# RWKV-7 state update without zero products, and MoE tail products in 64x64 tiles behind one step of the recurrence

## The chip, the cores and the metric

The kernel runs on one core of a Trainium2 chip. The metric is the device time of one execution in microseconds. An engine of the core runs its own list of instructions in order and waits for the others at semaphores: TensorE (PE; its weight loads are listed apart, as PEld), VectorE (DVE), ScalarE (ACT), GpSimd (POOL) and SyncE (SP), which issues nearly all the DMAs. PE multiplies a stationary operand, loaded by one instruction, with a moving one, streamed through by the next. A product that needs fewer than 128 rows or columns of the array can be put in a smaller tile (64x64, 32x64, ...), and products in different tiles run side by side. An fp32 product appears in the trace as two rows, each with its own weight load.

## The reference

Two blocks follow each other. The first is a recurrence over 768 steps, for 4 batches and 8 heads with a 40x40 state each:

```python
for t in range(S):
    y[:, :, t] = einsum('bhd,bhde->bhe', rt, state)
    Sa = einsum('bhde,bhe->bhd', state, at)
    state = state * wt - einsum('bhd,bhe->bhde', Sa, bt)
    state = state + einsum('bhd,bhe->bhde', vt, kt)
```

Its output, turned to 3072 tokens of 320 numbers, goes through the second block (the MoE): `h = x @ w_in` (320 to 2048), `g = h * cos(h)`, `g @ w_out` (2048 to 320). The second block's weights are float64 in memory; the kernel rounds them on the chip.

## The kernel before

The recurrence is cut into 24 chunks of 32 steps. With 4 batches this fills the 128 partitions: a block of 32 partitions for each batch (`blk`), or two halves of 64 partitions for the two heads of a pair (`half` takes the 40 used rows of each, `full` all 64). Within a chunk the recurrence is matrix algebra, and the chunk's main steps, in order, are t (transposes of the state, tile `sT`), q (the old state times r, tile `qps`), x (tile `x0ps`), s (tile `sps`) and z (the state update, tile `dps`, function `ch_z`). Steps v, k and g (tiles `vT`, `kT`, `gram`) prepare the next chunk from r, k and v; the p1 steps (`wT`, `aps`, `bT`, `nps`) and a triangular inverse on DVE prepare further ahead.

In z the result of one chunk is summed in four PSUM banks, one for each batch: products with kn (k divided by the decay), products with bn, and, ahead of both, eight products of a tile of bf16 zeros (`idle`), 64 wide and 288 columns long. They open the sum for all 64 partitions of each half: kn and bn products write 40 of the 64, and DVE (lines 736 and 743) reads all 128 partitions. Both kn and bn buffers are 64 columns wide with zeros in columns 40 to 63 (`kept("kn", ...)` fills the padding once).

The second block's work is cut into pieces: for each of 12 groups of 256 tokens and each of 4 slices of 512 hidden columns, a first half in two pieces, `first_a` and `first_b` (products in tile `ph`), then the cosine on ACT and DVE (lines 810 to 820), then the second half in two pieces (`second`, tile `po`). The 320 inputs are two full blocks of 128 rows and a tail of 64 rows. The tail's products (`tails`, with `w_in_tail`) use 64 rows and 128 columns of the array, for e = 0 and 1 in the upper and lower half of the rows, and write two PSUM banks.

The order is written out by hand: a list `segs` for each chunk names the steps, and a mark M stands where a piece of the MoE goes. `step` runs one step, notes in `G["small"]` whether it was one of the steps with small tiles (q, x, g, s, z and a few others), and issues what was put off (`later`), which holds the DMAs. `first_b` looks at that note: if the step just before it was small, the tail's products come first and the full ones after them; else the other way round. All PE products go through the helper `mm` at line 101, so groups are told apart by their tiles. Some products of zeros stand elsewhere only to keep PE going (`busy`, `spare`, FILL), and at chunk 19 there are 75 products of one column (`pad`).

Three waits hang on the places in question: ACT line 810 reads `ph` when a piece's first half is done; ACT line 654 copies q's result into `qz`, which x reads; DVE lines 736 and 743 read `dps` after z, POOL scales the state, and the next t reads it.

## Time and profile before

| what | value |
|---|---|
| time, median of 3 runs | 814.49 us (811.71 to 815.90) |
| the profiled execution's own time | 814.53 us |
| its span, first to last instruction | 812.8 us |
| mean granted TensorE clock | 0.975 |
| PE busy | 758.7 us (93%), 17,859 products |
| DVE / ACT / POOL busy | 485.8 / 387.1 / 199.4 us |
| products of zeros in z (`dps<-idle`) | 192 rows, 8.3 us busy |
| tail products (`ph<-xT,w_in_tail`) | 384 rows, 54.7 us busy |
| kn products (`dps<-vvm,kn`) | 1,536 rows, 21.6 us busy |
| reads of instructions (queue q8) | 140 packets of 16 KB |

A row of the list of groups gives line, engine, operation, output<-input, the shape, the count, the busy time in us and the mean of one in ns. A row of the timeline gives start and length in us of instructions of one kind merged together; since products side by side overlap, the time that a group takes is read from its start to the next group's start. "[0.45 <-issue]" behind a row says that the engine stood idle 0.45 us before it while it waited for nothing that the profile shows. The view of busy time by stretches gives for each engine its busy time in that stretch.

### The profile page before, as it was taken

Reading aid. Unit: us, or ns where it says so; the run is one execution under the profiler, and the core shown is the slowest. Engines: PE = TensorE matmul, PEld = TensorE weight load, DVE = VectorE, ACT = ScalarE, POOL = GpSimd, SP = SyncE. Lnnn points to the kernel's source line nnn. Section 1 sums busy time; section 2 is a strip of 40 time slices with the busy share of each in tenths; the row PEclk is TensorE's granted clock in tenths of the full one; section 3 lists DMA queues with packets and bytes.
Section 4 is the critical chain, followed back from the end, with each engine's and each line's share of the span. In section 5 each row is a group of like instructions: output and inputs, shape, how many; then the busy total and the mean of one; then the engine's idle time right before and its main releaser. Section 6 shows DMA issues by size and latency. Waiting matters only on the chain.

```text
span 812.8 us, 39682 instructions
## 1 busy us (share of the span) xinstructions
PE 758.7 (93%) x17859; PEld 582.0 (72%) x17859; DVE 485.8 (60%) x1025; ACT 387.1 (48%) x723; POOL 199.4 (25%) x354
## 2 busy tenths in 40 slices
PE   3678799799999999999999999999999999999997
PEld 2545477677777777777777777777777777777775
DVE  6948858855743797553895554994346873332231
ACT  1326577454454346446436535534635445363352
POOL 5215634330404230230330330331130222201000
PEclk9878699999999999999999999999999999999999
DMA  8656553344244324324214314223220212101000
GB/s 123 120 142 170 158 141 99 54 114 67 51 94 92 67 42 72 69 89 70 59 36 74 78 47 71 55 45 68 45 45 21 45 37 57 23 14 36 19 17 16
DMA packets 183304, 55.79 MB, mean 69 GB/s; under 512 B 157152, under 2 KB 178656, under 8 KB 183136
## 3 DMA queue, kind: packets, MB, share of 16 engines
q1 hardware_dynamic: 180560, 51.95, 29.5%
q8 instruction: 140, 2.29, 1.2%
q10 hardware_dynamic: 2320, 0.98, 0.6%
q0 software_dynamic: 256, 0.33, 0.2%
q14 instruction: 28, 0.23, 0.1%
HBM read 42.07 MB, written 11.14 MB: 65 GB/s over the span
## 4 chain that ended last, share of the span: by engine, by line
PE 68%; DVE 15%; DMA 4%; issue 4%; ACT 4%; SPq 3%; POOL 1%; DVEq 0%; ACTq 0%; POOLq 0%
PE ph L101 23%; PE po L101 19%; PE x0ps L101 4%; PE dps L101 3%; DVE inv_tmp L478 3%; SPq L152 3%; PE gram L101 3%; DVE inv L482 3%; PE vT L328 2%; DVE rw L393 2%; PE sps L101 2%; PE busy L101 2%; PE nps L101 2%; PE qps L101 2%; PE sT L638 1%
## 5 line engine op out<-in xcount | busy, mean ns | idle before, releaser
L101 PE MATMUL po<-w_out_sb,gT 128*128 128x320 f32 x768 | 223.3, 439 | 0.0
L101 PE MATMUL ph<-xT,w_in_sb 128*128 128x256 f32 x768 | 186.7, 388 | 1.5 <-DMA xT<-xd 1.5
L101 PEld LDWEIGHTS po<-w_out_sb,gT 128*128 128x128 f32 x768 | 140.2, 190 | 54.2 <-issue 1.7
L101 PEld LDWEIGHTS ph<-xT,w_in_sb 128*128 128x128 f32 x768 | 140.5, 191 | 30.0 <-issue 10.6
L810 ACT ACTIVATE turns<-ph,rnd 128x512 f32<-128x512 f32 x96 | 64.1, 686 | 151.7 <-PE ph L101 151.3
L812 DVE SCALAR_TENSOR_TENSOR turns<-turns,ph 128x512 f32<-128x512 f32 x96 | 64.0, 684 | 116.0 <-ACT turns L810 115.8
L820 DVE TENSOR_TENSOR gT<-ph,turns 128x512 f32<-128x512 f32 x96 | 65.8, 686 | 37.8 <-ACT turns L817 37.8
L737 POOL TENSOR_TENSOR qz<-qz,wc 128x160 f32<-128x160 f32 x92 | 42.0, 475 | 158.5 <-DVE qz L736 157.9
L817 ACT ACTIVATE turns<-turns,half_pi 128x512 f32<-128x512 f32 x96 | 69.3, 722 | 3.1
L816 ACT ACTIVATE turns<-turns 128x512 f32<-128x512 f32 x96 | 60.1, 627 | 19.1 <-DVE turns L812 19.1
L101 PE MATMUL ph<-xT,w_in_tail 64*128 64x256 f32 x384 | 54.7, 402 | 0.0
L482 DVE TENSOR_TENSOR inv<-inv,inv_tmp 128x31 f32<-128x31 f32 (+15 forms) x124 | 51.2, 413 | 4.3
L570 POOL COPY vp<-nat_v 128x320 f32<-128x320 f32 x24 | 11.7, 489 | 164.4 <-DMA nat_v<-in_v_dram 121.1
L478 DVE TENSOR_TENSOR inv_tmp<-u,inv 128x31 f32<-128x31 f32 (+15 forms) x124 | 48.5, 391 | 2.3
L736 DVE TENSOR_TENSOR qz<-dps,qz 128x160 f32<-128x160 f32 x92 | 29.1, 316 | 33.3 <-PE dps L101 33.2
L393 DVE RECIPROCAL rw<-nat_w 128x320 f32<-128x320 f32 x20 | 42.8, 2142 | 0.0
L642 ACT COPY s<-sT 128x512 f32<-128x512 f32 x46 | 24.5, 585 | 37.8 <-PE sT L638 37.8
L101 PEld LDWEIGHTS ph<-xT,w_in_tail 64*128 64x128 f32 x384 | 33.3, 186 | 9.3 <-issue 5.6
L101 PEld LDWEIGHTS <-idle 32*64 32x64 bf16 (+2 forms) x443 | 21.5, 101 | 24.3 <-issue 19.7
L748 POOL TENSOR_TENSOR yt<-yt,wb 128x512 f32<-128x512 f32 x24 | 31.6, 1316 | 22.4 <-DVE yt L743 22.4
L702 DVE TENSOR_TENSOR sm<-sps,su 128x128 f32<-128x128 f32 x48 | 11.7, 285 | 34.1 <-ACT sm L697 31.3
L394 POOL TENSOR_TENSOR bn<-nat_b,rw 128x320 f32<-128x320 f32 x22 | 19.8, 900 | 48.5 <-DVE rw L393 38.5
(136 smaller groups left out, 1126.7 us busy)
## 6 DMA issues: line engine op xcount, KB each, us to landing
words<-in_moe_w_in_dram SPq DMA_DIRECT2D x8, 512.0 KB
nat_k<-in_k_dram SPq DMA_DIRECT2D x96, 40.0 KB
nat_v<-in_v_dram SPq DMA_DIRECT2D x96, 40.0 KB
nat_r<-in_r_dram SPq DMA_DIRECT2D x96, 40.0 KB
xd<-yt SPq DMA_DIRECT2D x48, 80.0 KB
out_dram<-ot SPq DMA_DIRECT2D x24, 160.0 KB
nat_b<-in_b_dram SPq DMA_DIRECT2D x88, 40.0 KB
nat_a<-in_a_dram SPq DMA_DIRECT2D x80, 40.0 KB
```

Source lines behind the costliest of these rows:

```text
L101: nc.tensor.matmul(o, lhsT=lhsT, rhs=rhs, start=start, stop=stop, skip_group_check=True)
L393: nc.vector.reciprocal(rw, wn)
L478: nc.vector.tensor_tensor(tmp, u[:, j : j + 1, :j].to_broadcast([P, C - j, j]), x[:, j:, j : j + 1].to_broadcast([P, C - j, j]), ALU.mult,)
L482: nc.vector.tensor_tensor(x[:, j:, :j], x[:, j:, :j], tmp, ALU.subtract)
L736: nc.vector.tensor_tensor(z, pick(dp, 0, (2 * N72 + C, 2), (N72, 2), (1, D)), z, ALU.add)
L737: nc.gpsimd.tensor_tensor(z, z, wc.rearrange("p (f m b) -> p f m b", f=2, m=2)[:, :, :, bb] .unsqueeze(3).to_broadcast([P, 2, 2, D]), ALU. ...
L748: nc.gpsimd.tensor_tensor(yt.rearrange("p j b t -> p (j b) t"), yt.rearrange("p j b t -> p (j b) t"), wx, ALU.mult)
L810: nc.scalar.activation(n, u, ACTF.Identity, bias=rnd, scale=1.0)
L812: nc.vector.scalar_tensor_tensor(n, n, -ROUND, u, ALU.add, ALU.subtract)
L816: nc.scalar.activation(n, n, ACTF.Abs)
L817: nc.scalar.activation(n, n, ACTF.Sin, bias=half_pi, scale=-2.0 * math.pi)
L820: nc.vector.tensor_tensor(gT[:, 2 * e : 2 * e + 2].rearrange("p f t -> p (f t)"), us[e], ns[e], ALU.mult)
```

## The change

In `ch_z` the eight products of zeros go. The kn products take all 64 columns of kn (`DP` in place of `D`) and write all 64 partitions of a half, and those of j = 0 open the sum. The bn products stay 40 wide.

In `first_b`, where the step just before was q, each tail product 128 columns wide becomes two of 64 columns, in 64x64 tiles. `G["small"]` holds the kind of the step for that; after other small steps the tail's products stay as they were. In the instruction order of the changed program this is so in 16 places, and each has 8 products in place of 4.

The program's PE list goes from 36,027 instructions to 35,922: 384 fewer for the zeros, 256 more for the tails, 23 more waits. The order of everything else, on every engine and in the DMA queues, is the same. Constants (FILL, the 75 `pad` products) are not changed.

```diff
-        G["small"] = small
+        G["small"] = small and G["kind"]
...
-        for bb in range(B):
-            for e in range(2):
-                mm(
-                    ps[bb // 2][full[e], bb % 2, : 4 * N72], idle[blk[bb], :DP],
-                    pick(idle[blk[bb]], 0, (0, 4), (1, N72)), True,
-                )
         for s, n in ((0, kn_b[c % 2]), (1, bn_b[c % 7])):
             for j in range(4):
                 o = C - C * (j // 2)
                 for bb in range(B):
                     for e in range(2):
                         mm(
-                            ps[bb // 2][half[e], bb % 2, j * N72 : (j + 1) * N72],
-                            n[blk[bb], 2 * j + e, :D],
+                            ps[bb // 2][(half if s else full)[e], bb % 2, j * N72 : (j + 1) * N72],
+                            n[blk[bb], 2 * j + e, : D if s else DP],
                             sm[e][blk[bb], j, :] if s else vvm[c % 2][blk[bb], 2 * j + e, o : o + N72],
-                            False,
+                            not s and j == 0,
                         )
...
         def tails(fresh):
             for f in range(2):
                 for e in range(2):
-                    mm(
-                        phs[e][:, f, :], w_in_tail[full[e], j, f, :], xT[full[e], 2, :],
-                        fresh and e == 1 and f == 0, False,
-                    )
+                    for to in (full if G["small"] == "q" else [every]):
+                        mm(
+                            phs[e][to, f, :], w_in_tail[full[e], j, f, to], xT[full[e], 2, :],
+                            fresh and e == 1 and f == 0, False,
+                        )
...
+                    G["kind"] = "q" if seg is q else "other"
```

## The prediction

> **What bounds the kernel now.** I read the page's head first, then the chain that ended last, then busy time by stretches, and then the timeline around one q and one z.

> ```profile
> span 812.8 us, 39682 instructions
> PE 758.7 (93%) x17859; PEld 582.0 (72%) x17859; DVE 485.8 (60%) x1025; ACT 387.1 (48%) x723; POOL 199.4 (25%) x354
> PEclk9878699999999999999999999999999999999999
> ...
> PE 68%; DVE 15%; DMA 4%; issue 4%; ACT 4%; SPq 3%; POOL 1%; DVEq 0%; ACTq 0%; POOLq 0%
> ```

> ```profile
> 62.00:115.00 53.00, 44.51 (x1251) 30.12 (x1251) 41.23 (x74) 33.36 (x59) 29.03 (x29) 0.81 0.59 155
> 115.00:174.00 59.00, 53.09 (x1218) 42.30 (x1217) 44.86 (x82) 35.89 (x65) 22.59 (x35) 0.97 0.40 102
> 174.00:300.00 126.00, 119.77 (x3415) 94.05 (x3414) 78.79 (x176) 59.90 (x117) 27.72 (x55) 1.00 0.35 70
> 300.00:450.00 150.00, 148.00 (x3560) 115.60 (x3559) 97.67 (x212) 72.39 (x136) 34.84 (x63) 1.00 0.33 66
> 450.00:600.00 150.00, 148.99 (x3562) 116.74 (x3561) 92.12 (x196) 73.70 (x138) 38.25 (x71) 1.00 0.27 56
> ```

> In the stretches the first figure after the length is PE's busy time. Up to 174 us PE waits for loads, DVE and others, and the clock is not full; from 300 us it stands still for about 1% of the time, at full clock. A microsecond of PE saved after 174 us is a microsecond of the kernel, nearly; one saved before is perhaps none. Both edits touch PE alone. PE's busy share does not say what a group takes; that is read from start to start:

> ```profile
> 431.38 0.81 PE L101 MATMUL qps<-rT,s 40*40 40x32 f32 x64
> 432.13 1.14 PE L101 MATMUL ph<-xT,w_in_tail 64*128 64x256 f32 x8
> 433.19 1.99 PE L101 MATMUL ph<-xT,w_in_sb 128*128 128x256 f32 x8
> 435.02 0.60 PE L328 MATMUL kT<-ident,kn 128*128 128x128 f32 x4
> 435.55 0.88 PE L101 MATMUL x0ps<-vvm,ag 32*32 32x72 f32 x64
> 436.37 0.89 PE L101 MATMUL x0ps<-qz,aT 40*32 40x72 f32 x64
> 437.18 2.42 PE L101 MATMUL po<-w_out_sb,gT 128*128 128x320 f32 x8
> ...
> 447.36 0.33 PE L101 MATMUL dps<-idle 32*64 32x288 bf16 x8
> 447.51 0.86 PE L101 MATMUL dps<-vvm,kn 32*40 32x72 f32 x62
> ...
> 448.99 1.13 PE L101 MATMUL ph<-xT,w_in_tail 64*128 64x256 f32 x8
> 450.06 1.99 PE L101 MATMUL ph<-xT,w_in_sb 128*128 128x256 f32 x8
> 451.98 1.29 PE L101 MATMUL nps<-aT,bT 40*32 40x32 f32 x128
> ```

> **Term 1, the tails behind q (16 places).** Eight full products take 1.83 us when whole-array products follow (433.19 to 435.02), and 1.92 when small tiles follow (450.06 to 451.98). So a change of tile shape costs 0.09 us at the end of a group: the array drains. It costs again at the start, where the first weight load has no product to hide under:

> ```profile
> L101 PE MATMUL ph<-xT,w_in_tail x384: 375/376/481, 113.3 to 798.1; 64*128 64x256 f32 x192
> ```

> The slowest row is 481 ns against 376, 0.105 us more, and in the records of single instructions those are the first ones of a group. A tail group is then four steps of 0.216 us (the distance of full products' starts), two rows abreast, plus 0.10 at the start and 0.09 at the end: 1.06, as 432.13 to 433.19 shows. Behind q, whose tiles are 64x64, 64x64 tails change no shape: the drain behind q goes (0.09) and the load slides under q's last products (0.10). The four steps stay, now with four rows abreast; q's own rows run four abreast. Gain 0.19 us in each place, 3.0 in all. All 16 lie between 184 and 638 us. What was waiting gets its data earlier (ACT line 810); x reads q's copies 2.9 us after the last of them ends (432.26 plus 1.17 against 436.37), so 0.2 less slack there costs nothing. Bounds: nothing gained would be 0. If the eight extra rows queued one behind the other, each would cost what a row of the 75 `pad` products costs (632.40 to 634.35, 26 ns): 0.2 a place, 3.3 lost. Rows in different tiles of one step start 7 ns apart in the records, so I stay with 3.0 gained.

> **Term 2, the zeros in z (24 places).** They take 447.36 to 447.51, 0.15 us, and z as a whole 1.63. Against a gain of 0.15 speaks x: 128 rows of the same length, no zeros, also 1.63 (435.55 to 437.18), although with one change of tile shape inside. The single starts say why z may not shrink by the whole: its first 32 rows or so run at the array's pace (8 rows each 62 ns), then the queue of issued instructions is empty and the other 104 take 1.14 us, 11 ns each, as issue delivers them. Eight rows fewer are then 8 x 11 = 0.09 us. I take 0.09, between 0 and 0.15, as nearest to how the rows behind the zeros run. Four of the 24 places lie before 174 us; behind two more (207.5 and 239.8 us) PE waits in the same group for ACT (0.36 us) or just after it for DVE (1.4), and stands there longer instead. Left are 18 x 0.09 = 1.6 us; bounds 0 and 24 x 0.15 = 3.5.

> The kn products get wider. Output columns cost no streaming time; the weight load grows. Rows of loads:

> ```profile
> L101 PEld LDWEIGHTS ph<-xT,w_in_sb 128*128 128x128 f32 x768 | 140.5, 191 | 30.0 <-issue 10.6
> L101 PEld LDWEIGHTS dps<-vvm,kn 32*40 32x40 f32 x1536 | 20.2, 112 | 0.0
> ```

> Between 112 ns (40 columns) and 191 (128) lie about 133 for 64: 21 ns more. A tile gets one load each 62 ns, while the product before it streams; hidden, it costs nothing, and I take that. If it showed in each of the 8 rounds of a z, 0.17 us, 18 x 0.17 = 3.0 lost. [...]

> The first kn product now carries the waits that the first zero product carried (for the readers of the PSUM banks on ACT and DVE); 23 of them become instructions of their own. Behind them queues all of PE, but they ended at the same places before, so I count nothing.

> **Term 3, reads of instructions.** PE's program is read in 140 blocks of 16 KB, 256 instructions each:

> ```profile
> q8 instruction: 140, 2.29, 1.2%
> ...
> 443.99 0.69 PE L101 MATMUL sps<-x,rt 32*32 32x72 f32 x42 [0.45 <-issue]
> ```

> Such stops without a releaser (also 1.08 us before 129.90, 0.45 before 169.67, 0.47 before 200.18, and smaller ones, 3.9 us lost in all after 115 us) come in the records at PE's instruction numbers that are 194 above a multiple of 256, 1.3 to 1.5 us after a block has landed. A read starts some 1.0 to 1.3 us after the block before was entered and takes 0.9 to 1.6: where 256 instructions pass in under about 3.7 us, PE stops. The change moves the borders of all later blocks against the work, by up to 105 instructions. Laying the new order's borders over the old times gives a similar set of stops with one more near 205 us. I take 0.8 us lost; bounds 3.9 gained (none left) and 5 lost.

> **Sum.** 3.0 + 1.6 - 0.8 = 3.8 us gained. The profiled execution took 814.53 us, at the median of 814.49; 814.5 - 3.8 = 810.7.

> **Rivals.**
> - *Only the tails count.* z is paced by issue to its end, as x's equal 1.63 suggests, and the zeros were free: 3.0 - 0.8, time 812.3. Against it: fewer instructions have to be issued, too.
> - *Everything comes through.* 0.15 in 18 places, 3.0 for the tails, no new stops: 814.5 - 5.7 = 808.8; with the four early places and some stops gone, 807.
> - *Slower: the instruction blocks.* Each stop shown costs 0.45 to 1.08 us. If the borders fall before the dense stretches (g, x, s with 256 instructions in 1.2 to 1.6 us), about one in 20 of the 110 blocks after 174 us stopping for 1 us more would eat the 4.6 gained; at 9 new stops of 1 us the time is 819. It decides from 5 new ones on. For it: every border behind the first z moves. Against it: most blocks take 5 us or more to pass.
> - *The change does not do what it says*, if the four 64x64 rows of a step do not run abreast: with 0.2 lost in each place, 814.5 + 3.3 - 1.6 + 0.8 = 817.

> **How the numbers follow.** Half a per cent, 4.1 us, is about what a measurement of this kernel tells from no change: its three runs alone span 811.7 to 815.9. The forecast's own range, with terms 2 and 3 varied, is 808.5 to 812.5, chance 0.48, and its middle lies just inside half a per cent, so I split it 0.23 faster, 0.25 same. Only the tails: 0.22, same. Everything: 0.18, faster. Blocks: 0.08, rows not abreast: 0.04, of which 0.02 together still fall within half a per cent. Faster 0.41, same 0.49, slower 0.10. The range takes in all but the ends of these: 806.5 to 815.8. A stretch of half clock more or less before 174 us (one is 3.4 us long) would move the time by up to 1.7 us, and lies in it.

> **What would show it.** Right: tails behind q start about 0.1 us sooner behind q's last row, in eights of four, and the group takes about 0.95 us; no row of 481 ns left among them; z from first kn row to the next group 1.54 in place of 1.63; stops without releaser 4 to 5 us in all. Wrong: tails behind q at 1.06 or more; kn's rows more than 62 ns a round; z at 1.63 or at 1.48; new stops of a microsecond where g or x begins.

## The result, and the profile after

| | before | after |
|---|---|---|
| time, median of 6 runs | 813.91 us (811.71 to 815.90) | 825.28 us (819.46 to 830.80) |
| ratio | | 1.0137, 95% interval 1.0108 to 1.0167 |
| the profiled execution's own time | 814.53 us | 822.18 us |

The change makes the kernel 1.4% slower. The page's head, and the shares of the chain that ended last, for the kernel after:

```profile
span 820.5 us, 39577 instructions
...
PE 757.4 (92%) x17795; PEld 577.4 (70%) x17795; DVE 486.1 (59%) x1025; ACT 386.9 (47%) x723; POOL 199.3 (24%) x354
...
PEclk9968799999899999999999999999999999999999
...
PE 68%; DVE 15%; issue 5%; DMA 5%; ACT 5%; POOL 1%; SPq 1%; DVEq 0%; ACTq 0%; POOLq 0%
```

Sixty-four products fewer, PE busy 1.3 us less, and the span 7.7 us longer: PE does not work longer, it stands longer. Busy time by stretches says where:

```profile
115.00:174.00 59.00, 50.66 (x1162) 39.90 (x1149) 44.27 (x82) 35.81 (x65) 24.40 (x37) 1.00 0.43 112
174.00:300.00 126.00, 115.77 (x3126) 89.85 (x3125) 71.23 (x156) 55.06 (x108) 25.53 (x51) 0.96 0.35 68
300.00:450.00 150.00, 147.28 (x3593) 114.78 (x3594) 103.44 (x225) 73.85 (x139) 33.57 (x60) 1.00 0.32 63
450.00:600.00 150.00, 146.67 (x3598) 114.28 (x3583) 87.20 (x190) 73.53 (x139) 33.93 (x65) 1.00 0.29 58
```

Between 174 and 300 us PE was busy 119.8 us before and is busy 115.8 now, and the clock, 1.00 before, is 0.96. The edits' own places look as they should. PE's timeline around one q and one z of after:

```profile
438.01 0.81 PE L101 MATMUL qps<-rT,s 40*40 40x32 f32 x64
438.65 1.14 PE L101 MATMUL ph<-xT,w_in_tail 64*64 64x256 f32 x16
439.72 1.99 PE L101 MATMUL ph<-xT,w_in_sb 128*128 128x256 f32 x8
...
453.46 0.95 PE L101 MATMUL dps<-vvm,kn 32*64 32x72 f32 x62
...
455.92 0.70 PE L101 MATMUL dps<-sm,bn 32*40 32x72 f32 x41 [1.27 <-issue]
456.55 1.14 PE L101 MATMUL ph<-xT,w_in_tail 64*128 64x256 f32 x8
```

q and its tails take 1.71 us where they took 1.81; this z, alone, is stopped for 1.27 us in its middle by nothing that the profile shows. Such stops fill PE's list of waits after 174 us (who waited, for what, us in total, times, longest):

```profile
PE gram L101 <- issue: 3.0, 2, 2.1
...
PE dps L101 <- issue: 2.0, 2, 1.3
PE nps L101 <- issue: 1.8, 1, 1.8
PE below L101 <- issue: 1.6, 1, 1.6
...
PE sps L101 <- issue: 0.4, 1, 0.4
```

The same list for the kernel before:

```profile
PE below L101 <- issue: 0.5, 1, 0.5
PE sps L101 <- issue: 0.4, 1, 0.4
```

8.8 us against 0.9. All seven stand at PE's instruction numbers 194 above a multiple of 256, or one beside it, 1.2 to 1.6 us after a read of a 16 KB instruction block has landed. Such a place, where PE goes from one block of 256 instructions to the next, is called a border below. Two of them are followed by something dearer. PE's timeline of after:

```profile
198.34 0.31 PE L101 MATMUL below<-rn,noff 32*32 32x16 f32 x14 [1.57 <-issue]
198.58 3.51 PE L101 MATMUL ph<-xT,w_in_sb 128*128 128x256 f32 x8
...
218.27 0.19 PE L101 MATMUL gram<-rT,vT 40*32 40x32 f32 x1 [2.14 <-issue]
```

The eight `ph` products take 3.51 us where before they take 2.00 (196.76): the clock has halved. Busy time in windows of 3.41 us (the last three figures are the clock, the DMA share and GB/s):

```profile
171.57:174.98 3.41, 2.10 (x82) 1.74 (x81) 0.24 (x1) 2.05 (x4) 3.35 (x7) 1.00 0.60 211
174.98:178.39 3.41, 2.63 (x68) 2.19 (x68) 0.81 (x1) 1.89 (x5) 0.35 (x1) 1.00 0.29 74
195.46:198.87 3.41, 1.83 (x130) 1.57 (x130) 0.29 (x1) 0.59 (x2) 0.00 (x0) 1.00 0.42 69
198.87:202.28 3.41, 3.41 (x27) 2.29 (x33) 0.00 (x0) 0.10 (x1) 0.00 (x0) 0.50 0.39 73
215.94:219.35 3.41, 1.11 (x31) 0.86 (x18) 0.42 (x1) 0.37 (x1) 2.73 (x4) 1.00 0.18 53
219.35:222.76 3.41, 2.92 (x75) 2.48 (x73) 3.22 (x4) 0.00 (x0) 0.00 (x0) 0.50 0.23 61
222.76:226.17 3.41, 3.41 (x11) 2.78 (x10) 3.27 (x6) 1.07 (x2) 2.66 (x3) 0.50 0.51 79
```

The two stops that fall into one window (1.83 us busy, 1.11) are followed by half clock. The stop of 1.81 us ahead of 175.76 us, cut in two by an edge (2.10 and 2.63 busy), is not; PE's timeline has it as:

```profile
175.76 0.69 PE L101 MATMUL nps<-aT,bT 40*32 40x32 f32 x58 [1.81 <-issue]
```

**Where the time went.** Laid group by group on the kernel before, from 170 us on, after loses 9.4 us: gained about 3.5 at z and behind q, lost 3.9 in the three half-clock windows (`ph` at 198.6 us 1.52, `sT` and `ph` at 221 and 223 us 0.83 and 1.52), and the rest, some 9 by subtraction, most of it in the stops listed. Up to 170 us it is 1.8 us ahead. That figure varies: e2, e6 and e7 below, whose program up to 165 us is that of before, are 2.4 to 6.6 us ahead of the same profile there. 9.4 - 1.8 = 7.6 is the difference of the two profiled times.

### The profile page after: what moved, and what is told of

Read it like the earlier page. It is cut to its first block, busy times and chain, and to the rows that moved or that the text cites. A ratio compares the mean times of both kernels' runs of the same rounds, so it can differ in the third digit from the quotient of the medians.

```text
span 820.5 us, 39577 instructions
## 1 busy us (share of the span) xinstructions
PE 757.4 (92%) x17795; PEld 577.4 (70%) x17795; DVE 486.1 (59%) x1025; ACT 386.9 (47%) x723; POOL 199.3 (24%) x354
## 3 DMA queue, kind: packets, MB, share of 16 engines
q8 instruction: 140, 2.29, 1.2%
## 4 chain that ended last, share of the span: by engine, by line
PE 68%; DVE 15%; issue 5%; DMA 5%; ACT 5%; POOL 1%; SPq 1%; DVEq 0%; ACTq 0%; POOLq 0%
PE ph L101 22%; PE po L101 20%; PE x0ps L101 4%; PE dps L101 3%; PE gram L101 3%; PE vT L328 2%; DVE rw L393 2%; PE sps L101 2%; DVE inv_tmp L478 2%; DVE inv L482 2%; PE qps L101 2%; PE nps L101 2%; PE busy L101 1%; PE sT L638 1%; DVE turns L807 1%
## 5 line engine op out<-in xcount | busy, mean ns | idle before, releaser
L101 PE MATMUL po<-w_out_sb,gT 128*128 128x320 f32 x768 | 223.3, 439 | 0.0
L101 PE MATMUL ph<-xT,w_in_sb 128*128 128x256 f32 x768 | 188.0, 390 | 1.2 <-DVE gT L815 1.2
L101 PEld LDWEIGHTS po<-w_out_sb,gT 128*128 128x128 f32 x768 | 140.2, 190 | 54.3 <-issue 1.7
L101 PEld LDWEIGHTS ph<-xT,w_in_sb 128*128 128x128 f32 x768 | 141.3, 192 | 31.0 <-issue 12.9
L101 PE MATMUL ph<-xT,w_in_tail 64*128 64x256 f32 (+1 forms) x512 | 54.0, 393 | 0.0
L101 PEld LDWEIGHTS ph<-xT,w_in_tail 64*128 64x128 f32 (+1 forms) x512 | 31.7, 160 | 9.2 <-issue 5.6
L626 ACT COPY vvm<-gram 128x256 f32<-128x256 f32 x24 | 8.8, 368 | 46.8 <-DVE ag L621 46.4
```

Of the source, the lines that this page charges most:

```text
L101: nc.tensor.matmul(o, lhsT=lhsT, rhs=rhs, start=start, stop=stop, skip_group_check=True)
```

## The experiments

Theory: the edits gain what was predicted; the moved borders of PE's 256-instruction blocks cost more than that. Rivals: the new rows themselves are dear; the start-up is upset. "Numbers" are places in PE's list of instructions; a one-column product is two of them.

### e1 and e2: each edit alone

e1 has the change in `ch_z` only, e2 the change in `tails` only.

e1 against before:

```diff
-        for bb in range(B):
-            for e in range(2):
-                mm(
-                    ps[bb // 2][full[e], bb % 2, : 4 * N72], idle[blk[bb], :DP],
...
-                            n[blk[bb], 2 * j + e, :D],
+                            n[blk[bb], 2 * j + e, : D if s else DP],
...
-                            False,
+                            not s and j == 0,
```

e2 against before:

```diff
-        G["small"] = small
+        G["small"] = small and G["kind"]
...
+                    for to in (full if G["small"] == "q" else [every]):
+                        mm(
+                            phs[e][to, f, :], w_in_tail[full[e], j, f, to], xT[full[e], 2, :],
...
+                    G["kind"] = "q" if seg is q else "other"
```

> Only the first edit: the products of zeros are gone, kn's products are 64 columns wide, the tails are as before. Theory (block borders): PE gains 0.08 us in each z, about 1.5 in all, but PE's instruction numbers run 62 to 76 behind those of before between 174 and 240 us, nearly as in the changed kernel (60 to 45 behind), so that stops of 1.5 us and more come there too and are paid a second time by a stretch of half clock: 816 to 823 us. Rival 1 (the rows themselves: wider kn products are dear in a way that the groups' start-to-start times do not show): also slower, 820 to 825. Rival 2 (only the start-up, before 115 us, moved): 812 to 815. The trace tells the first two apart: stops without a releaser and half clock between 174 and 245 us for the theory, slower z groups for rival 1.

> Only the second edit: tails behind q in 64x64 tiles, the products of zeros are kept. Theory (block borders): nothing moves before the first of the 16 places at 185 us, so the numbers are those of before up to there and 16 to 48 ahead between 186 and 260 us; the groups gain 0.17 us in each place, 2.7 in all, and the two long stops of the changed kernel near 196 and 216 us are not there: 810 to 814 us. Rival 1 (the 64x64 tails themselves are dear): 818 to 825, with the loss spread over all 16 places. Rival 2 (the tails bring nothing, only the start-up counts): 813 to 815.

Measured: e1 823.33 us, ratio 1.0138 (1.0090 to 1.0185), the whole loss; e2 816.73 us, 1.0046 (1.0013 to 1.0080), where 810 to 814 was expected. In e1's trace 15 of the 20 z after 174 us are 0.08 to 0.15 us shorter than before, as they should be; the loss is stops (2.1 us ahead of 177 us, 0.8 of 201, 1.3 of 221, 1.7 of 312, 1.1 of 659 and two of 0.5) and five windows of half clock after 174 us. So its rows are not what is dear. In e2 the long stops near 196 and 216 us are absent, as expected, but a stop of 1.34 us ahead of 334.66 us and half clock behind it (1.7 us) take back more than the 2.2 us that the tails gain. That was not expected: a move by 80 numbers, as at that place, is not harmless either. The profiled execution, at 813.36 us, is 3.4 us faster than e2's median, so that its trace shows only a part of the miss.

### e3 and e4: the borders moved, the edits not; and the reverse

e3 against before; e4 is the changed kernel with the same lines and `bare = c >= 4`:

```diff
+        bare = c < 4
         for bb in range(B):
             for e in range(2):
+                if not bare:
...
+                        wide = bare and not s
...
-                            n[blk[bb], 2 * j + e, :D],
+                            n[blk[bb], 2 * j + e, : DP if wide else D],
...
-                            False,
+                            wide and j == 0,
```

> The kernel before, with the products of zeros removed in the first four z alone (chunks 0 to 3, all before 174 us, where PE waits for others anyway). After them the work is that of the kernel before, group for group, but its instruction numbers are 61 smaller to the end. Theory (block borders): the borders lie between 174 and 240 us where the changed kernel has them, the long stops at 196 and 216 us are back with the half clock behind them, with nothing gained for it: 818 to 824 us. Rival (the edits' own rows cost the time): four of 24 z changed, 813 to 815.5.

> The changed kernel, with the products of zeros kept in the first four z alone (chunks 0 to 3). After them the work is that of the changed kernel, but its instruction numbers are those of before, 0 to 32 ahead, up to 655 us. Theory (block borders): the stops of 1.7 and 2.3 us at 196 and 216 us and the two stretches of half clock go, and the gains of 20 z and 16 tail groups stay: 808 to 812 us, faster than both kernels. Rival (the edits' own rows cost the time): 20 of 24 z and all tails are as in the changed kernel, 822 to 826.

Measured: e3 822.46 us, 1.0136 (1.0087 to 1.0186): the whole loss of the change with four of its 40 places, all of them before 174 us. e4 812.36 us, 1.0006 (0.9979 to 1.0033): the loss gone, with 36 of the 40 places changed. e3's busy time by stretches, with the half-clock windows cut out:

```profile
174.00:212.50 38.50, 34.62 (x1081) 26.53 (x1079) 22.92 (x58) 16.37 (x34) 5.85 (x13) 1.00 0.28 52
212.50:222.70 10.20, 8.88 (x92) 7.67 (x93) 7.15 (x13) 1.07 (x2) 2.96 (x4) 0.50 0.37 76
222.70:246.60 23.90, 22.46 (x730) 17.92 (x728) 9.75 (x21) 13.76 (x26) 2.92 (x9) 1.00 0.44 103
246.60:250.00 3.40, 3.40 (x24) 2.27 (x13) 1.36 (x3) 0.35 (x1) 3.40 (x6) 0.50 0.18 52
```

Its first half clock begins at 212.46 us, within a stop of 2.93 us that ends at 213.26 us ("aps", waiting for nothing shown). With the work untouched after 170 us, PE's numbers alone cost 12.6 us there. What e4 does not show is the gain: it was expected at 808 to 812 us.

### e5 to e8: nothing but numbers

Products of zeros of one column, ahead of z of chunk 3, in columns of the PSUM bank that nobody reads: 20 or 31 in the changed kernel (e5, e8), 64 or 128 in the kernel before (e6, e7).

```diff
         ps = [at("dps") for _ in range(2)]
         sm = G["sm"]
+        for i in range(20 if c == 3 else 0):
+            mm(ps[i % 8 // 4][full[i % 2], i // 2 % 2, 511:512], idle[blk[i // 2 % 4], :DP], idle[blk[i // 2 % 4], :1], True)
```

> The changed kernel with 20 products of zeros of one column each (40 instructions) ahead of z of chunk 3, at 166 us; nothing else is changed, and they add work (20 x 11 = 0.2 us). From there on the numbers are 23 below to 1 above those of before in place of 62 to 30 below. Theory (block borders): laying the borders over the starts, with each block ready 3.8 us after the one before was entered, leaves about 1 us of stops after 174 us (8.8 in the changed kernel, 2.0 before) and at most one stretch of half clock (1.6): 808 to 812 us. Rival (removing the early products of zeros upsets the start-up, before 160 us, and e4 mended that): nothing is mended here, 822 to 826.

> The kernel before with 64 products of zeros of one column each (128 instructions, half a block) ahead of z of chunk 3, at 168 us. The added work is 64 x 11 = 0.7 us. Theory (block borders): the borders lie half a block off, the worst place for them; the same working gives 11 to 18 us of stops after 174 us and several stretches of half clock of 1.6 us each: 826 to 840 us. Rival (it is the start-up or the edits' own rows): 814 to 816.

> The kernel before with 128 such products (256 instructions, a whole block) in the same place. Theory (block borders, 256 instructions long): twice the added work of the run with 64, 1.4 us, but the borders fall where they fell before: 813 to 816 us, far below the run with 64. Rival (what costs is the number of added instructions itself): twice what the run with 64 costs.

> The changed kernel with 31 products of one column (62 instructions) in that place: from there on the numbers are those of the run with the early products of zeros kept, within 2, but the first four z are those of the changed kernel. Theory (block borders): as that run, 809 to 813 us; 0.5 to 2 us behind the run with 20, whose borders lie better. Rival (start-up): 822 to 826.

| | added to | us | ratio to before |
|---|---|---|---|
| e5 | after, 40 numbers | 810.62 | 0.9985 (0.9957 to 1.0013) |
| e8 | after, 62 numbers | 811.58 | 1.0007 (0.9982 to 1.0032) |
| e6 | before, 128 numbers | 825.41 | 1.0198 (1.0135 to 1.0262) |
| e7 | before, 256 numbers | 818.98 | 1.0075 (1.0038 to 1.0111) |

Twenty useless products make the changed kernel 1.5% faster; the start-up, which is that of after, is not the cause. Half a block costs the kernel before 13 us for 0.7 us of work, a little less than expected. A whole block costs 7, not the 2 or less that was expected, but not twice 13 either. Its trace shows where they are lost:

```profile
165.80 1.37 PE L101 MATMUL dps<-idle 32*64 32x1 bf16 x136
166.96 0.82 PE L101 MATMUL dps<-vvm,kn 32*40 32x72 f32 x60
...
170.29 1.27 PE L101 MATMUL dps<-sm,bn 32*40 32x72 f32 x63 [2.45 <-issue]
171.49 4.43 PE L101 MATMUL po<-w_out_sb,gT 128*128 128x320 f32 x8
```

136 products pass in 1.2 us, the block behind them has not come (2.45 us), and half clock follows (`po` 4.43 us against 2.42): 4.4 us between 168 and 173 us of before. From there to the end e7 loses 1.3 us more, a half-clock window at 247 us (1.7) included, while e6, half a block off, loses 11 from 173 us on. The period of 256 holds.

### e9 and e10: a wait filled

Both add 8 one-column products at z of chunk 3 to the changed kernel, and 16 products at the end of z of chunk 5, where PE waits for DVE: 192 columns wide in e9, one in e10.

```diff
+        if c == 5:
+            for _ in range(16):
+                mm(G["po", 0][:, DM : DM + 192], idle, pick(idle, 0, (0, 2), (1, 96)), False)
```

> The changed kernel with 8 one-column products ahead of z of chunk 3 (borders 46 to 30 numbers before those of before up to 240 us), and with 16 products of 192 columns, whose sums nobody reads, behind z of chunk 5, where PE stands 1.2 to 1.5 us for DVE (a stretch of half clock followed there, at 238 to 247 us, in eight of the ten profiles so far). Theory: the borders are as good as in the run with 20 small products, and the filled wait lets no half clock begin there, about 1.3 us less than the same kernel with the wait unfilled: 808 to 811 us. Rival (half clock has nothing to do with the wait in the window before): not faster than the unfilled one, or 1 us slower for the work added.

> The same kernel, instruction for instruction, but each of the 16 products behind z of chunk 5 has one column in place of 192, so that PE stands still there as before. Theory: the same borders and stops, and half clock for 3.4 us or more after the wait at about 240 us in most executions: 809.5 to 812.5 us, 1.3 us behind the filled one. Rival: the same time as the filled one or less.

Measured: e9 811.99 us, 1.0000 (0.9968 to 1.0033); e10 810.96 us, 0.9971 (0.9942 to 1.0001). The profiled execution of e9 has no half clock between 92 us and its last 4 us, that of e10 three windows. Over twelve runs each the filled kernel is not faster, so by time the expectation failed, and what the filling is worth stays open.

### e11 to e14: where the gain is

In e4, e5, e8, e9 and e10 the loss is gone, but 3 to 4 us gained on PE do not appear. In e5 and e8 a new stop shows where some of it went: 1.49 us ahead of 238.74 us with one window of half clock behind it, and 1.28 us ahead of 237.62 us with two. e11 has both edits only where the numbers can be held within 16 of before's, z of chunks 7 to 18 and tails of chunks 8 to 19; e12 starts at chunk 4. e13 is e11 with 69 in place of 75 `pad` products, so that from 632 us on the numbers are exactly those of before. e14 is e13 with the tails behind q cut to 64 of 256 columns; it leaves out three quarters of these products.

e11 against after, with the lines of e3 that use `bare`; e12 has 4 in place of 7 and 5 in place of 8:

```diff
+        bare = 7 <= c < 19
...
-                    G["kind"] = "q" if seg is q else "other"
+                    G["kind"] = "q" if seg is q and 8 <= c < 20 else "other"
```

e13 against e11:

```diff
-        N_PAD = {0: 0, 19: 75}
+        N_PAD = {0: 0, 19: 69}
```

e14 against e13:

```diff
+                        cut = slice(0, 64 if G["small"] == "q" else 2 * P)
-                            phs[e][to, f, :], w_in_tail[full[e], j, f, to], xT[full[e], 2, :],
+                            phs[e][to, f, cut], w_in_tail[full[e], j, f, to], xT[full[e], 2, cut],
```

> Both edits, but only in a stretch where PE hardly ever waits: no products of zeros in z of chunks 7 to 18 (from 297 us), 64x64 tails behind q of chunks 8 to 19 (to 639 us); the rest is the kernel before. A z takes 16 numbers away and the next tails give 16 back, so that no border moves by more than 16 anywhere, and nothing at all moves before 297 us. Theory (the edits save what the groups show, and only the borders took it back): 12 x 0.08 + 12 x 0.17 = 3.0 us less than before, 808.5 to 810 us, ratio 0.996. Rival (the gains on PE are given back later, to waits for other engines, whatever the borders do): 0.999 or more.

> The same from chunk 4 on (z at 208 us, tails at 222 us): 15 z and 15 tail groups, borders again within 16 numbers of those of before, but now also in the stretch from 208 to 250 us, where PE often stands for DVE, ACT or a block. Theory: 13 x 0.08 (two z have a wait behind or in them that takes it back) + 15 x 0.17 = 3.6 us less than before, less up to 1 us of new stops there: 808.5 to 810.5 us. Rival (gains given back): 0.999 or more.

> Both edits in chunks 7 to 19 alone, as in the run from 297 us on, and 69 in place of 75 one-column products at 632 us, so that from there to the end every instruction has exactly the number that it has in the kernel before, and up to 297 us too. Theory A (the groups save 3.0 us and only displaced borders take it back): 809.0 us, ratio 0.996, and no stop over 0.3 us that before does not have at 650 to 670 us. Theory B (a microsecond saved on PE between 297 and 639 us is given back later to something that the borders have no part in): ratio 0.999 or more.

> The same kernel, but the tails behind q in chunks 8 to 19 stream 64 of their 256 columns: three quarters of these products are left out, and the output for those tokens is not the reference's. Instruction for instruction it is the same program. Each of the 12 groups falls from 0.86 us of streaming to what issue allows for 32 rows, some 0.35 us: 12 x 0.5 = 6 us of PE less. Theory A: the time falls by 6 us against the same kernel with whole tails, to about 803 us, ratio 0.989. Theory B: by clearly less, 0.993 or more.

| | us | ratio to before |
|---|---|---|
| e11 | 812.17 | 1.0012 (0.9988 to 1.0035) |
| e12 | 815.20 | 1.0028 (1.0000 to 1.0055) |
| e13 | 809.92 | 0.9960 (0.9937 to 0.9984) |
| e14 | 806.01 | 0.9905 (0.9879 to 0.9931) |

e11's trace gains 2.6 us on before's between 285 and 640 us, and loses 1.1 in two tail groups at 650 and 665 us; the second is a stop at a border 12 numbers from where before has it (from PE's waits between 640 and 690 us):

```profile
PE ph L101 <- issue: 0.5, 1, 0.5
```

e12 loses 0.4 and 1.5 us at the same two. e13, whose numbers there are before's, has none, and is 0.4% faster than before, as theory A had it: the one version of the study that does the whole work and is shown to beat both kernels. (Its six `pad` products fewer are 6 x 26 ns, under 0.2 us of that.) Its ratio lies below e11's without overlap, though the two ran on different chips. e14 gains 0.63 us in ten of 12 places and 0.70 and 0.77 in two, 7.8 on PE, more than the 6 expected; against e13's trace 5.3 of them are left, since `sps` now waits 1.0 us twice for DVE, and a stop of 0.9 has come at 634 us. From PE's waits between 300 and 660 us in e14:

```profile
PE sps L101 <- DVE x L680: 2.0, 2, 1.0
...
PE gram L101 <- issue: 0.9, 1, 0.9
```

The median falls by 3.9 us against e13. So one half to two thirds of what PE saves in that stretch reaches the end at this size. Theory A's 6 was too high. Theory B is out for e13, whose interval ends below its 0.999; for e14 it is in part right: 2.0 us went to waits for DVE, and the interval just reaches its 0.993.

e12 shows something else. Its program is that of before up to 208 us, and so is e11's. PE's timeline of e12, and then of e11, at one and the same border:

```profile
195.45 0.49 PE L101 MATMUL below<-rn,noff 32*32 32x16 f32 x36 [1.65 <-issue]
195.88 3.20 PE L101 MATMUL ph<-xT,w_in_sb 128*128 128x256 f32 x8
```

```profile
192.95 0.72 PE L101 MATMUL below<-rn,noff 32*32 32x16 f32 x62
193.60 1.99 PE L101 MATMUL ph<-xT,w_in_sb 128*128 128x256 f32 x8
```

The same instructions with the same numbers: a stop of 1.65 us and half clock in one execution, neither in the other. What differs is the read. In e12 the read of that block (queue q8) began 2.9 us after PE had passed the border before, in e11 0.9 us after; the reads themselves took 0.9 and 1.2 us. Over the 16 traces, 115 to 700 us, the median of this delay is 0.97 us, and half of 1,352 reads lie between 0.82 and 1.20. Where the borders lay set which stops could come (e3, e6 against e4, e5); how long one got differed from execution to execution (1.65 us in e12, none in e11). This may be a part of the 10 us over which the runs of the kernel before spread beside e11 and e12 (807.3 to 817.5); no run isolates it.

## Why the prediction was wrong

- **What bounds the kernel**: PE after 174 us, as said. "Nearly" was too much for larger savings: e14 gave back a third to a half, to DVE and to a stop.
- **Term 1, tails behind q**: right in kind. q to tails falls from 0.745 to 0.634 us in 14 of 16 places. The tails' own time falls from 1.064 to 1.003 in ten, so that 0.17 is gained there, 0.10 in four, 0.02 in two: 2.2 us in place of 3.0. In the six that gain less, and in none of the ten, one or two waits stand as instructions of their own in PE's list within 0.11 us of the tails' first row; there the first four rows start 67 or 131 ns apart from first to last in place of 20, and the group takes 0.07 or 0.13 us longer. The prediction had no term for that. The rival that the rows do not run abreast is out: in the ten, neighbours start 7 ns apart.
- **Term 2, zeros**: right. 15 of the 20 z after 174 us gain 0.077 to 0.080 each, 1.2 us in place of 1.6. kn's loads take 133 ns, the value that was interpolated, and hide, as taken. The wider products take no longer either: kn's rows have a median of 221 ns at 64 columns, as at 40 before.
- **Term 3, instruction blocks**: this is the step that failed. "I take 0.8 us lost; bounds 3.9 gained and 5 lost" measured about 8 us in stops (8.8 against 0.9 after 174 us), and 3.9 more for the half clock behind two of them. The stops' place in the program (194 above a multiple of 256), the time after the landing and the direction were right. Wrong were the sizes: the stops were priced by the four that before shows, 0.45 to 1.08 us, while four of the new ones stopped PE for 1.3 to 2.1. And half clock was allowed for only before 174 us. Laying the new borders over the old times gave one stop more, near 205 us; there were five more, and a stop's length, taken as fixed, varies by over a microsecond between executions (e11, e12). What made the sizes wrong is the delay of the reads, "some 1.0 to 1.3 us after the block before was entered": ahead of six of the seven stops in after it was 2.0 to 5.0 us. So blocks stopped PE that would have taken 3.7 to 5.7 us to pass, over the 3.7 us that the prediction allowed. Only the seventh stop, at 218.27 us, came by the prediction's working (a delay of 1.2 us, and 256 instructions in 1.3 us). In the trace of before, too, two of the four stops had delays of 1.9 and 2.6 us. Why a read begins late stays open.
- **Rivals**: "the instruction blocks" at 0.08 was the one that came, with seven stops of 0.4 to 2.1 us after 174 us and a time 6 us above its 819; the half clock that it left out cost 3.9 us in the profiled execution. What spoke against it, that most blocks take 5 us or more to pass, is beside the point: seven of the 110 were enough.
- **What would show it**: "new stops of a microsecond", named as the mark of a wrong prediction, were there, at g but also in nps, below and z. Of the signs of being right, those at the edits' own places came as well: tails 0.11 us sooner behind q, no row over 427 ns among them, z at 1.53 us; the tail group took 1.00 to 1.14 us, not 0.95.

## What to carry to other kernels

On a kernel like this one, with a list of 36,027 instructions on PE, adding or removing a few of them early can change everything behind (e3, 61 numbers: ratio 1.0136; e5, 40 numbers: 0.9985 where after has 1.0137): first move the numbers alone (useless products in a pause, half a block and a whole one), and learn what that costs. Then judge an edit in a version that keeps the numbers of before, as e13 does; without it, e1 would have been read as "kn's wide products are dear". A wait on PE like the one of 1.57 us in after is to be priced with the half clock that may follow it, here 0.8 to 1.7 us a window.
